# All score groups mirrored from two or more groups back, in the space of weights that are loaded later, and v loaded in eight parts

## The chip, the cores and the metric

The kernel runs on one core of a Trainium2 chip. The metric is device time in microseconds (us), the median of several executions. The core has a matrix engine (PE, whose weight loads are shown as PEld), a vector engine (DVE), a scalar engine (ACT), a general engine (POOL) and a sync engine (SP). SP and POOL also issue DMAs, which 16 DMA engines carry out; those of SP and of POOL go through queues of their own. PSUM is the memory that PE writes its sums to, SBUF the working memory.

## The reference

Eight batches of 2816 rows go through a gated attention, and the result, taken as 22528 tokens, through a mixture of experts:

```python
scores = (1.0 / S) * np.matmul(z, z.transpose(0, 2, 1))   # z: (8, 2816, 64)
attn = np.maximum(scores, 0.0) ** 2
x = u * np.matmul(attn, v)                                # u, v: (8, 2816, 256)
...
h_dense = np.maximum(x @ w1_dense, 0.0)
y_dense = h_dense @ w2_dense
expert_idx = np.argmax(x @ w_gate, axis=1)                # 8 experts
...
y_moe[mask] = gate_w[mask, None] * (np.maximum(x[mask] @ w1[e], 0.0) @ w2[e])
out = y_dense + y_moe
```

Since the scores are z times its own transpose, the matrix `attn` is symmetric: its block (k, i) is the transpose of block (i, k).

## The kernel before, in words

The order of PE, ACT, DVE and SP is written out when the program is built: the code keeps a clock `now` in estimated us, and a small planner (`offer`, `best`, `give`, `run`) hands each vector step to ACT, DVE or POOL by estimated cost and due time. On the chip the engines then follow that order and wait on semaphores only.

**Blocks and groups.** A batch has 22 blocks of 128 rows (`nK = 22`), cut into six groups of 2, 4, 4, 4, 4 and 4 blocks (indices 0 to 5 here). A group's buffer `A[n]` holds `attn` for all 22 key blocks against the group's own blocks, in bf16. There are three such buffers, taken in turn, so group n + 3 reuses the buffer of group n, and scores can run at most two groups ahead (`ahead`, L468).

**Scores.** `scores` (L368) makes two key blocks against the four blocks of a group: two matmuls of 64 x 512, one on the upper and one on the lower half of the array (L383; for the two-block group four key blocks, in four matmuls of 64 x 256). `relu` (L390) then scales and clips from PSUM to a float32 tile `r` (L398 on ACT or L400 on DVE), and a second pass squares into `A` (L411 on ACT, L413 on DVE). PSUM has four pairs of banks for scores, outputs and routing.

**Mirrors.** For `far[n] = [n - 2]`, within a batch, the key blocks that are the columns of group n - 2 are not computed: `far_steps` (L436) issues DMA transposes from `A[n - 2]` on SP (L446), one DMA for each block of group n, with up to four 128 x 128 blocks in each. There are 16 such DMAs in a batch, 128 in all, with 2 x 4 + 3 x 16 = 56 blocks per batch.

**Values.** `av` (L525) makes the output of two blocks i and i + 1 in two passes over the 22 key blocks, in pairs of 64-row matmuls (L552). Between matmuls it lets `fill` run a score call of a group further on. In a group's first pass the key blocks come in the order in which they are expected to be ready. Between the passes `swap_rows` (L503) puts two score calls, or two dummy matmuls `touch` (L496), since the halves of the array change roles there. Every seventh pair of matmuls may issue a mirror DMA (L559). When both passes are done DVE multiplies by u into `pays` (L579), and SP transposes that into `xT` (L581).

**The rest on the queues.** The calendar (`later`, `soon`, L980 to L1008) places steps at ticks, two for each pair of blocks, 22 for a batch: the load of the next batch's z at tick 1, its turning at 6 and 7 (SP), four loads of v at ticks 10, 12, 14 and 16 (`load_v`, L122: a DVE memset of one element, L128, then POOL's DMA, L129), and the weights of the experts (`weights`, L252) three to a batch from batch 2 on. u is loaded by SP (L146) two pairs ahead. Logits (`lg`, L607) for 11 blocks are made five ticks after the last of them is due, from `xT`. POOL scatters each routed block to DRAM (L697).

**Weights.** `wall` holds the weights of the eight experts in SBUF, 2048 elements of each partition for each expert: 1024 for w1, 1024 for w2. They are read only after attention, when the expert stage runs (L909, L912, L917, L932, L933), with DVE copying an expert's weights out of `wall` (L897).

Of the kernel before, what the change touches and what calls it, by code (L numbers as in the profile page):

```python
# [10 lines left out]
BF = mybir.dt.bfloat16  # L11
# [4 lines left out]
P = 128  # L16
# [3 lines left out]
def kernel(  # L20
# [39 lines left out]
    WD = 2 * F + 4 * D  # L60
# [8 lines left out]
    def pool(name, bufs, **kw):  # L69
        return ctx.enter_context(tc.tile_pool(name=name, bufs=bufs, **kw))  # L70
# [3 lines left out]
    aA = pool("aA", 3)  # L74
# [28 lines left out]
    def load_z(b):  # L103
        z_of[b] = zpool.tile([P, nK, dq], BF, name="zr", bufs=1)
        nc.vector.memset(z_of[b][:, 0, 0:1], 0.0)
        nc.gpsimd.dma_start(out=z_of[b][:], in_=z[b].rearrange("(p k) d -> p k d", p=P))

    def turn_z(b, k0, k1):

        if k0 == 0:  # L110
            zn_of[b] = zpool.tile([P, nK, 2, dq], BF, name="zn", bufs=1)
            zT_of[b] = zpool.tile([P, nK, P], BF, name="zT")
        nc.vector.tensor_copy(  # L113
            zn_of[b][:, k0:k1, :, :],
            z_of[b][:, k0:k1, :].unsqueeze(2).to_broadcast([P, k1 - k0, 2, dq]))
        nc.sync.dma_start_transpose(
            out=zT_of[b][:, k0:k1, :],
            in_=zn_of[b][:, k0:k1].rearrange("p k h d -> p (k h d)"))
        if k1 == nK:
            z_there.add(b)  # L120

    def load_v(b, h, parts, gate=True):  # L122
        if h == 0:
            v_of[b] = zpool.tile([P, nK, D], BF, name="vb")
        src = v[b].rearrange("(p k) d -> p k d", p=P)
        k0, k1 = h * nK // parts, (h + 1) * nK // parts
        if gate:
            nc.vector.memset(v_of[b][:, k0, 0:1], 0.0)  # L128
        nc.gpsimd.dma_start(out=v_of[b][:, k0:k1, :], in_=src[:, k0:k1, :])  # L129
        free["pool"] = max(free["pool"], now[0]) + 0.8  # L130


    now = [0.0]
# [130 lines left out]
    A = {}  # L264
    groups = []
    for b in range(B):
        i = 0
# [61 lines left out]
    def until(cond):  # L329

        while cond() is None:
            pick = best()
            assert pick is not None
            now[0] = max(now[0], pick[0][0])
            give(pick)
        now[0] = max(now[0], cond())
        run(now[0])
# [3 lines left out]
        run(now[0])  # L341


    left, far, key_at = {}, {}, {}
    for n, (b, i0, w) in enumerate(groups):
        far[n] = [m for m in (n - 2,) if m >= 0 and groups[m][0] == b]
        turned = {k for m in far[n] for k in range(groups[m][1], groups[m][1] + groups[m][2])}
        ks = [k for k in range(0, nK, 2) if k not in turned]

        left[n] = [tuple(ks[x:x + 4 // w]) for x in range(0, len(ks), 4 // w)]  # L350

    def open_group(n):
        if n not in A:
            A[n] = aA.tile([P, nK, 4 * P], BF, name="A", tag="A")

    def room(n):

# [3 lines left out]
    def take_pair():  # L361
        return pairs.pop(0)[1]
# [68 lines left out]
    def can_turn(n, m):  # L431
        _, i0, w = groups[n]
        ts = [key_at.get((m, k)) for k in range(i0, i0 + w)]
        return None if None in ts else max(ts)

    def far_steps(a):  # L436

        n = a + 2
        if n >= len(groups) or far[n] != [a]:
            return []  # L440
        (b, i0, w), (_, j0, wj) = groups[n], groups[a]

        def step(i):
            assert n - 1 in A
            open_group(n)
            nc.sync.dma_start_transpose(out=A[n][:, j0:j0 + wj, i * P:(i + 1) * P],  # L446
                                        in_=A[a][:, i0 + i, :wj * P])
            if i == w - 1:
                for j in range(wj):
                    key_at[n, j0 + j] = now[0] + 10.0  # L450

        return [(a, lambda i=i: step(i)) for i in range(w)]

    jobs = []

    def fill(n, force=False):

        if jobs and jobs[0][0] <= now[0] and room(1):
            jobs.pop(0)[1]()
            return True  # L460
        m = ahead(n)
        busy = sum(1 for op in todo if op[0] in (1, 4))
        if m is not None and room(1) and busy <= (4 if n < 2 else 2):
            scores(m, left[m].pop(0))
            return True
        return False

    def ahead(n):  # L468

        for m in range(n, min(n + 3, len(groups))):  # L470
            if left[m]:
                return m if groups[m][0] in z_there else None

    def v_at(n, k):

        return 3.3 + 2.6 * (4 * k // nK) if n == 0 else 0.0

    def need(n, k):

        while max(key_at.get((n, k), 9e9), v_at(n, k)) > now[0]:  # L480
            if fill(n):
                continue
            pick = best()
            ts = [t for t, _ in pairs if t > now[0]]
            ts += [max(key_at[n, k], v_at(n, k))] if (n, k) in key_at else []
            assert pick is not None or ts
            if pick is not None and (not ts or pick[0][0] <= min(ts)):
                now[0] = max(now[0], pick[0][0])
                give(pick)
            else:  # L490
                now[0] = min(ts)
        run(now[0])

    turning = []

    def touch(x):  # L496

# [27 lines left out]
    def av(n, i, between):  # L525
        b, i0, w = groups[n]
        if i == i0:
            turning.extend(far_steps(n))
        keep[0] = 0
        if n == 0 and i == i0:  # L530

            fill(n)
            need(n, 0)
        until(lambda: pairs[0][0] if pairs else None)
        ox = take_pair()
        o = banks(ox, "o")
        for p in range(2):
            rest = list(range(nK))
            for x in range(nK):
                k = rest[0]  # L540
                if i == i0 and p == 0:

                    k = min(rest, key=lambda k: (max(key_at.get((n, k), 9e9), v_at(n, k)), k))
                    need(n, k)
                rest.remove(k)
                if n == 0 and i == i0 and p == 0 and x in (12, 14, 16):
                    load_u(2 * (x - 12) // 2, gate=True)
                for h in range(2):
                    r = slice(h * dq, (h + 1) * dq)
                    j = p ^ h  # L550
                    c = (i + j - i0) * P
                    nc.tensor.matmul(out=o[:, j, 0:D], lhsT=A[n][r, k, c:c + P],  # L552
                                     rhs=v_of[b][r, k, :], start=(p == 0 and x == 0),
                                     stop=(p == 1 and x == nK - 1))
# [430 lines left out]
    def soon(t, fn, dur=0.07):  # L985
        at(t, lambda: offer(now[0], 3, {"dve": (dur, lambda eng: fn())}))
# [19 lines left out]
    for e in range(E):  # L1006
# [62 lines left out]
    for q in range(nQ - 2):  # L1069
        t = starts[q + 1] - 1 + LAG  # L1070
# [40 lines left out]
    for s in range(NT - MAYBE + 2):  # L1111
# [4 lines left out]
        if s % 3 == 1 and waiting:  # L1116
# [5 lines left out]
    n = nc.values_load(used[0:1, 0:1], min_val=0, max_val=NH,  # L1122
                       skip_runtime_bounds_check_because="made by the table")
# [34 lines left out]
```

## Time and profile before

| | us |
|---|---|
| median of 3 runs | 882.46 |
| lowest and highest run | 880.53, 889.76 |
| the profiled execution | 887.47 |
| its span, first to last instruction | 885.8 |
| granted PE clock, mean over the span | 0.994 |

The profiled execution is 5.0 us above the median, and 1.7 us of it lie outside the span. In the profile L12 is line 12 of the kernel; a group is written line, engine, operation, out<-in, shape and count, then busy us, mean ns of one, and the engine's idle time ahead of it with what ended it. A name with q (SPq, POOLq) is an engine's queue of instructions that issue DMAs. The DMA share is packet time over 16 engines; packet times can overlap, so it can pass 1.

### The profile page before, as it was taken

To read this page: it belongs to the slowest core of one execution; us is meant where nothing else is said; L and a number is where in the kernel's file an instruction comes from. 1 tells how busy PE (TensorE), PEld (TensorE's weight loads), DVE (VectorE), ACT (ScalarE), POOL (GpSimd) and SP (SyncE) were. 2 spreads that over 40 slices of the span, in tenths; PEclk is the share of its full clock that TensorE was granted. 3 is DMA by queue.
4 is the path that set the end of the run, shared out by engine and by line. 5 is a ranking of instruction groups with operands and counts; after the bars stand their busy time and mean duration, and the time that the engine had idled before them with its cause. 6 is when DMAs were issued, how large, how long until landed. Compare 5 with 4: busy or idle time off the path is not lost.

```text
span 885.8 us, 30592 instructions
## 1 busy us (share of the span) xinstructions
PE 864.5 (98%) x12257; PEld 759.7 (86%) x12257; DVE 701.2 (79%) x1320; ACT 738.6 (83%) x913; POOL 485.2 (55%) x532
## 2 busy tenths in 40 slices
PE   8999999999998999999999999999999999999996
PEld 5788888898886888888888888888888888889996
DVE  7999999998996999999998997656665445546664
ACT  7999998998996998998998997477777777777774
POOL 8203343434533534434434544488888888887665
PEclk9999999999999999999999999999999999999998
DMA  6795997998898899899899896555565555544333
GB/s 148 148 174 117 146 185 145 172 174 170 153 165 168 154 181 190 127 197 198 131 196 172 151 159 112 103 133 128 129 132 122 117 120 121 123 113 110 97 100 82
DMA packets 257871, 127.64 MB, mean 144 GB/s; under 512 B 225470, under 2 KB 232894, under 8 KB 257728
## 3 DMA queue, kind: packets, MB, share of 16 engines
q1 hardware_dynamic: 230112, 70.24, 47.6%
q0 software_dynamic: 27616, 55.44, 29.2%
q8 instruction: 96, 1.57, 0.8%
q14 instruction: 47, 0.39, 0.2%
HBM read 61.54 MB, written 37.16 MB: 111 GB/s over the span
## 4 chain that ended last, share of the span: by engine, by line
PE 73%; DVE 7%; issue 6%; POOL 6%; DMA 4%; ACT 3%; SPq 0%; POOLq 0%; DVEq 0%; ACTq 0%
PE o L552 37%; PE h_ps L909 14%; PE yy L917 13%; PE s L383 8%; POOL out_dram L935 5%; DMA xT<-pays 3%; DVE r L400 2%; DVE A L413 2%; ACT A L411 1%; POOL A L413 1%; PE lg L607 1%; ACT r L398 1%; DVE pays L579 1%; DMA out_dram<-ring,ix 1%; DVE zn L113 1%
## 5 line engine op out<-in xcount | busy, mean ns | idle before, releaser
L552 PE MATMUL o<-vb,A 64*128 64x256 bf16 x7744 | 493.7, 270 | 2.6 <-POOL A L413 1.8
L552 PEld LDWEIGHTS <-A 64*128 64x128 bf16 x7744 | 408.1, 94 | 53.9 <-POOL A L413 3.0
L697 POOL DMA_INDIRECT xs<-pays,pi x176 | 196.9, 1119 | 271.1 <-DVE pi L695 207.1
L398 ACT ACTIVATE r<-s 128x1024 f32<-128x1024 f32 x274 | 270.0, 1011 | 26.1 <-PE s L383 22.1
L411 ACT ACTIVATE A<-r 128x1024 bf16<-128x1024 f32 (+1 forms) x257 | 261.3, 1042 | 5.3 <-DMA A<-A 2.7
L912 ACT ACTIVATE ring<-h_ps 128x1024 bf16<-128x1024 f32 x180 | 183.9, 1023 | 89.2 <-PE h_ps L909 87.3
L413 DVE TENSOR_TENSOR A<-r 128x1024 bf16<-128x1024 f32 x167 | 201.8, 1221 | 5.8 <-DMA A<-A 4.0
L400 DVE TENSOR_SCALAR r<-s 128x1024 f32<-128x1024 f32 (+1 forms) x158 | 190.5, 1214 | 4.3 <-POOL A L413 1.8
L933 DVE SCALAR_TENSOR_TENSOR ring<-yy,me,ring 128x256 f32<-128x256 f32 x180 | 86.8, 482 | 123.0 <-ACT ring L932 86.3
L935 POOL DMA_INDIRECT out_dram<-ring,me x140 | 146.4, 1046 | 39.8 <-issue 23.5
L383 PE MATMUL s<-zT 64*128 64x512 bf16 (+1 forms) x944 | 157.9, 359 | 1.6 <-ACT zT L192 0.6
L917 PEld LDWEIGHTS <-ring 128*128 128x128 bf16 x1440 | 140.0, 98 | 16.2 <-issue 0.3
L917 PE MATMUL yy<-w2d,ring 128*128 128x256 bf16 x720 | 108.0, 273 | 0.1
L917 PE MATMUL yy<-ring 128*128 128x256 bf16 x720 | 108.0, 273 | 0.0
L909 PE MATMUL h_ps<-ring,w1d 128*128 128x256 bf16 x720 | 93.3, 273 | 0.8 <-DVE pays L579 0.8
L909 PE MATMUL h_ps<-ring 128*128 128x256 bf16 (+1 forms) x880 | 93.7, 253 | 0.0
L897 DVE COPY ring<-wall 128x2048 bf16 x110 | 80.7, 748 | 8.6 <-DVE ring L933 4.2
L909 PEld LDWEIGHTS <-ring 128*128 128x128 bf16 x880 | 74.3, 98 | 6.8
L909 PEld LDWEIGHTS <-w1d 128*128 128x128 bf16 x720 | 70.1, 98 | 9.0 <-issue 1.0
L579 DVE TENSOR_TENSOR pays<-o,ut 128x512 bf16<-128x512 f32 x88 | 60.3, 685 | 17.6 <-PE o L552 17.1
L383 PEld LDWEIGHTS <-zT 64*128 64x128 bf16 x944 | 58.0, 94 | 16.0 <-issue 3.4
L932 ACT COPY ring<-yy 128x256 f32<-128x256 f32 x180 | 66.1, 367 | 1.8 <-PE yy L917 1.8
(120 smaller groups left out, 358.0 us busy)
## 6 DMA issues: line engine op xcount, KB each, us to landing
ut<-in_u_dram SPq DMA_DIRECT2D x88, 256.0 KB
vb<-in_v_dram POOLq DMA_DIRECT2D x16, 384.0 KB
vb<-in_v_dram POOLq DMA_DIRECT2D x16, 320.0 KB
wall<-in_moe_w_dram POOLq DMA_DIRECT2D x16, 256.0 KB
xs<-pays,pi POOLq DMA_INDIRECT x176
zr<-in_z_dram POOLq DMA_DIRECT2D x7, 352.0 KB
out_dram<-ring,me POOLq DMA_INDIRECT x140
A<-A SPq DMA_TRANSPOSE x128
```

The lines of the kernel that those rows point to most:

```text
L383: nc.tensor.matmul(out=s[:, h, y * c:(y + 1) * c], lhsT=zT[r, k + h, :], rhs=zT[r, i0:i0 + w, :], start=True, stop=True)
L398: nc.scalar.activation(r[:, :, :c], s[:, :, :c], AF.Relu, scale=1.0 / S)
L400: nc.vector.tensor_scalar(out=r[:, :, :c], in0=s[:, :, :c], scalar1=1.0 / S, scalar2=0.0, op0=ALU.mult, op1=ALU.max)
L411: nc.scalar.activation(a, r, AF.Square)
L413: (nc.gpsimd if eng == "pool" else nc.vector).tensor_mul(a, r, r)
L552: nc.tensor.matmul(out=o[:, j, 0:D], lhsT=A[n][r, k, c:c + P], rhs=v_of[b][r, k, :], start=(p == 0 and x == 0), stop=(p == 1 and x == nK - 1))
L697: ins = nc.gpsimd.indirect_dma_start(out=xs, out_offset=bass.IndirectOffsetOnAxis(ap=pi[:], axis=0), in_=pays[:, g % (2 * G), 0:ROW].bitca ...
L909: nc.tensor.matmul(out=h_ps[:, f, hs, :], lhsT=w1(c, f), rhs=xT[:, hs, c, :], start=(c == 0), stop=(c == 1))
L912: nc.scalar.activation(h, h_ps[:].rearrange("p f h t -> p f (h t)"), AF.Relu)
L917: nc.tensor.matmul(out=y[:, k, :], lhsT=h[:, f, j * P:(j + 1) * P], rhs=w2(f), start=(f == 0), stop=(f == 3))
L933: nc.vector.scalar_tensor_tensor(out=ys, in0=y[:, 1, :], scalar=me[:, j, 0:1], in1=yd, op0=ALU.mult, op1=ALU.add)
L935: ins = nc.gpsimd.indirect_dma_start(out=out, out_offset=bass.IndirectOffsetOnAxis(ap=ids[j], axis=0), in_=ys, in_offset=None, bounds_chec ...
```

## The change

A group is now mirrored from every earlier group of its batch that is two or more back. The mirrors from exactly two back go into the group's own buffer, as before; those from further back go to slots in `wall` that belong to the experts 3 to 7, whose weights come later. Batch 6 uses the slots of experts 7 and 6 alone, batch 7 none. One DMA now carries all the blocks between two groups, 16 (8 from the two-block group), and the layout of a mirrored piece is one run of blocks. A score call of the group that will reuse a buffer waits, in the planner, until the mirrors from that buffer are issued and expected to be read (`read_at`), and two mirror DMAs are spaced by `turn_at`. `A` of the two-block group is packed. z is loaded one tick sooner, v in eight parts at ticks 13 to 20, and the weights at the ends of the batches from 3 on.

```diff
+    spare = wall[:].rearrange("p e w -> p (e w)")
+    mirror = {(2, 5): (E - 1) * WD, (1, 5): (E - 2) * WD, (1, 4): (E - 3) * WD,
+              (0, 4): (E - 4) * WD, (0, 5): (E - 4) * WD + 8 * P, (0, 3): (E - 5) * WD + 2 * F}
+
+    def slots(b):
+        if b < B - 2:
+            return list(mirror)
+        return [(2, 5), (1, 5)] if b == B - 2 else []
...
-        far[n] = [m for m in (n - 2,) if m >= 0 and groups[m][0] == b]
+        far[n] = [m for m in range(max(n - 5, 0), n - 1)
+                  if groups[m][0] == b and (m == n - 2 or (m % 6, n % 6) in slots(b))]
...
     def open_group(n):
         if n not in A:
-            A[n] = aA.tile([P, nK, 4 * P], BF, name="A", tag="A")
+            while turning and turning[0][0] <= n - 3:
+                turning.pop(0)[1]()
+            A[n] = aA.tile([P, nK, 4 * P], BF, name="A", tag="A")[:]
+            w = groups[n][2]
+            if w < 4:
+                A[n] = A[n].rearrange("p k c -> p (k c)")[:, :nK * w * P]
+                A[n] = A[n].rearrange("p (k c) -> p k c", k=nK)
...
+    def turned_to(a, n):
+        _, j0, wj = groups[a]
+        w = groups[n][2]
+        if a == n - 2:
+            flat = A[n].rearrange("p k c -> p (k c)")
+            return flat[:, j0 * w * P:(j0 + wj) * w * P]
+        x = mirror[a % 6, n % 6]
+        return spare[:, x:x + w * wj * P]
+
+    def block(n, k, c):
+        _, i0, w = groups[n]
+        for a in far[n]:
+            _, j0, wj = groups[a]
+            if j0 <= k < j0 + wj:
+                x = c * wj + k - j0
+                return turned_to(a, n)[:, x * P:(x + 1) * P]
+        return A[n][:, k, c * P:(c + 1) * P]
...
     def far_steps(a):
-        def step(i):
-            assert n - 1 in A
-            open_group(n)
-            nc.sync.dma_start_transpose(out=A[n][:, j0:j0 + wj, i * P:(i + 1) * P],
-                                        in_=A[a][:, i0 + i, :wj * P])
...
+        _, j0, wj = groups[a]
+        def step(n):
+            _, i0, w = groups[n]
+            if n == a + 2:
+                assert a + 1 in A
+                open_group(n)
+            nc.sync.dma_start_transpose(
+                out=turned_to(a, n).rearrange("p (x c) -> p x c", c=P),
+                in_=A[a][:, i0:i0 + w, :].rearrange("p k c -> p (k c)"))
+            turn_at[0] = now[0] + 0.17 * w * wj
+            read_at[a] = now[0] + 1.5 + 0.19 * w * wj
+            for j in range(wj):
+                key_at[n, j0 + j] = now[0] + 7.0
+
+        return [(a, lambda n=n: step(n), n) for n in range(a + 2, min(a + 6, len(groups)))
+                if a in far[n]]
...
             if left[m]:
+                if m == n + 2 and (turning and turning[0][0] <= m - 3 or read_at.get(m - 3, 0.0) > now[0]):
+                    return None
                 return m if groups[m][0] in z_there else None
...
-                    nc.tensor.matmul(out=o[:, j, 0:D], lhsT=A[n][r, k, c:c + P],
+                    nc.tensor.matmul(out=o[:, j, 0:D], lhsT=block(n, k, i + j - i0)[r],
...
-                if x % 7 == 3 and turning:
-                    t = can_turn(turning[0][0] + 2, turning[0][0])
+                if x % 7 == 3 and turning and turn_at[0] <= now[0]:
+                    t = can_turn(turning[0][2], turning[0][0])
...
-            soon(t + 1, lambda b=b: load_z(b + 1))
-            soon(t + 6, lambda b=b: turn_z(b + 1, 0, nK // 2), 0.4)
-            soon(t + 7, lambda b=b: turn_z(b + 1, nK // 2, nK), 0.4)
-            for h in range(4):
-                soon(t + 10 + 2 * h, lambda b=b, h=h: load_v(b + 1, h, 4))
+            soon(t, lambda b=b: load_z(b + 1))
+            soon(t + 5, lambda b=b: turn_z(b + 1, 0, nK // 2), 0.4)
+            soon(t + 6, lambda b=b: turn_z(b + 1, nK // 2, nK), 0.4)
+            for h in range(8):
+                soon(t + 13 + h, lambda b=b, h=h: load_v(b + 1, h, 8))
 
-    ts = [b * nK + x for b in range(1, B) for x in (0, 5, 18)][3:]
+    ts = [b * nK + x for b in range(3, B - 2) for x in (15, 18, 21)]
+    ts += [(B - 2) * nK + x for x in (14, 16, 18, 20, 21)]
+    ts += [(B - 1) * nK + x for x in (0, 5, 10, 15)]
```

More of the change, by code (lines that the diff above doesn't have):

```diff
@@ L434, in can_turn @@
         return None if None in ts else max(ts)
-    def far_steps(a):
[L438 to L441, printed above, removed]
-        def step(i):
-            assert n - 1 in A
-            open_group(n)
-            nc.sync.dma_start_transpose(out=A[n][:, j0:j0 + wj, i * P:(i + 1) * P],
-                                        in_=A[a][:, i0 + i, :wj * P])
[L448 to L452, printed above, removed]
+    def turned_to(a, n):
[14 more added lines that the diff above has]
+        return A[n][:, k, c * P:(c + 1) * P]
+    def far_steps(a):
+        _, j0, wj = groups[a]
[13 more added lines that the diff above has]
+                if a in far[n]]
+    turning = []
+    turn_at = [0.0]
+    read_at = {}
     jobs = []
@@ L492, in need @@
         run(now[0])
-    turning = []
     def touch(x):
@@ L550, in av @@
                     j = p ^ h
-                    c = (i + j - i0) * P
-                    nc.tensor.matmul(out=o[:, j, 0:D], lhsT=A[n][r, k, c:c + P],
+                    nc.tensor.matmul(out=o[:, j, 0:D], lhsT=block(n, k, i + j - i0)[r],
                                      rhs=v_of[b][r, k, :], start=(p == 0 and x == 0),
@@ L996 @@
         if b + 1 < B:
-            soon(t + 1, lambda b=b: load_z(b + 1))
-            soon(t + 6, lambda b=b: turn_z(b + 1, 0, nK // 2), 0.4)
-            soon(t + 7, lambda b=b: turn_z(b + 1, nK // 2, nK), 0.4)
-            for h in range(4):
-                soon(t + 10 + 2 * h, lambda b=b, h=h: load_v(b + 1, h, 4))
-    ts = [b * nK + x for b in range(1, B) for x in (0, 5, 18)][3:]
+            soon(t, lambda b=b: load_z(b + 1))
[6 more added lines that the diff above has]
+    ts += [(B - 1) * nK + x for x in (0, 5, 10, 15)]
+    assert len(ts) == 2 + 2 * E
     soon(ts.pop(0), lambda: dense(w1d, moe_w1_dense, 2))
```

## The prediction

> **What bounds the kernel now.** I read the page first, then the stages, then single matmuls. The page:
>
> ```profile
> span 885.8 us, 30592 instructions
> ...
> PE 864.5 (98%) x12257; PEld 759.7 (86%) x12257; DVE 701.2 (79%) x1320; ACT 738.6 (83%) x913; POOL 485.2 (55%) x532
> ...
> PE 73%; DVE 7%; issue 6%; POOL 6%; DMA 4%; ACT 3%; SPq 0%; POOLq 0%; DVEq 0%; ACTq 0%
> PE o L552 37%; PE h_ps L909 14%; PE yy L917 13%; PE s L383 8%; POOL out_dram L935 5%; DMA xT<-pays 3%; DVE r L400 2%; DVE A L413 2%; ACT A L411 1%; POOL A L413 1%; PE lg L607 1%; ACT r L398 1%; DVE pays L579 1%; DMA out_dram<-ring,ix 1%; DVE zn L113 1%
> ```
>
> PE is busy 98% of the span, and 73% of the chain that ended last is PE. A stage of attention (busy us of PE, PEld, DVE, ACT, POOL with their counts, then granted clock, DMA share and rate):
>
> ```profile
> 320.00:395.00 75.00, 74.91 (x1277) 65.73 (x1275) 72.07 (x126) 70.25 (x78) 32.45 (x34) 1.00 1.04 175
> ```
>
> There PE, DVE (72.07 of 75), ACT (70.25) and the DMA engines (share 1.04) are all nearly full. Which one sets the pace is seen in PE's order of time (start, length, engine, line):
>
> ```profile
> 354.04 2.80 PE L552 MATMUL o<-vb,A 64*128 64x256 bf16 x48
> 356.66 0.40 PE L383 MATMUL s<-zT 64*128 64x512 bf16 x2
> 356.88 0.40 PE L552 MATMUL o<-vb,A 64*128 64x256 bf16 x4
> 357.09 0.17 PE L499 MATMUL d<-ones 64*128 64x8 bf16 x1
> 357.11 0.64 PE L383 MATMUL s<-zT 64*128 64x512 bf16 x4
> 357.58 1.49 PE L552 MATMUL o<-vb,A 64*128 64x256 bf16 x24
> ```
>
> 48 value matmuls take 356.66 - 354.04 = 2.62 us: two run side by side on the halves of the array, and each pair costs 0.109 us. A score call of a four-block group costs 356.88 - 356.66 = 0.22 us (two calls: 357.58 - 357.11 = 0.47). Nothing is idle between, so PE's own work is the attention's time. The Trainium skill ("Perfetto Trace Analysis", section Identifying the Most-Contended Engine) says that matmul busy time is a bad measure of PE's headroom and that weight-load busy time is a good one; by that, the 65.73 of 75 would leave 12% in PE. The spacing decides against it here.
>
> **Scores removed.** Per batch, group 3 takes 2 more key blocks from mirrors, group 4 takes 6 and group 5 takes 10: 18 key blocks, in 9 calls of two. Batches 0 to 5 lose 9 calls, batch 6 loses 4, batch 7 none: 58 of 432 (the built order has 944 - 828 = 116 score matmuls fewer). On PE 58 x 0.216 = 12.5 us, all on the path. What goes with them on the other engines:
>
> ```profile
> L398 ACT ACTIVATE r<-s 128x1024 f32<-128x1024 f32 x268 | 266.5, 1020 | 25.4 <-PE s L383 21.5 <-POOL A L413 1.0 <-DVE A L413 0.6
> L411 ACT ACTIVATE A<-r 128x1024 bf16<-128x1024 f32 x251 | 257.9, 1052 | 5.3 <-DMA A<-A 2.7 <-DVE r L400 1.3 <-DVE vb L128 0.8
> L413 DVE TENSOR_TENSOR A<-r 128x1024 bf16<-128x1024 f32 x166 | 201.1, 1224 | 5.8 <-DMA A<-A 4.0 <-ACT r L398 1.0
> L400 DVE TENSOR_SCALAR r<-s 128x1024 f32<-128x1024 f32 x156 | 189.1, 1221 | 4.1 <-POOL A L413 1.6 <-PE s L383 1.2
> ```
>
> 116 passes of 1.02 to 1.22 us, some 130 us over two engines, which only gives them slack.
>
> **Swaps without scores.** With fewer calls to spread, more passes end with no score to run, and two dummies stand in. The built order has 16 such pairs of dummies, against 8:
>
> ```profile
> 345.15 0.42 PE L499 MATMUL d<-ones 64*128 64x8 bf16 x2
> 345.42 0.83 PE L552 MATMUL o<-vb,A 64*128 64x256 bf16 x12
> ```
>
> 345.42 - 345.15 = 0.27 us each: 8 x 0.27 = 2.2 us back.
>
> **Mirrors added.** SP issues 70 mirror DMAs for 128, but they carry 128 blocks per batch for 56. Their load:
>
> ```profile
> q1 hardware_dynamic: 230112, 70.24, 47.6%
> ```
>
> 0.476 x 885.8 us x 16 / 230112 = 29.3 ns of one engine per packet. A block is 32 KB in 256-byte packets, so 128 of them: 0.234 us of all 16 engines (an estimate). 72 more blocks cost 16.9 us per batch, nearly all in the first six block pairs of a batch. Batch 4's first six, before:
>
> ```profile
> 299.00:305.00 6.00, 6.00 (x105) 5.44 (x101) 5.66 (x10) 5.97 (x7) 3.32 (x3) 1.00 0.92 151
> 305.00:311.00 6.00, 6.00 (x113) 5.09 (x111) 5.90 (x11) 5.89 (x8) 2.66 (x2) 1.00 1.08 196
> 311.00:317.00 6.00, 6.00 (x103) 4.84 (x101) 5.79 (x11) 6.00 (x7) 2.75 (x3) 1.00 1.03 170
> 317.00:323.00 6.00, 6.00 (x107) 5.19 (x103) 5.44 (x16) 5.71 (x7) 1.49 (x2) 1.00 1.48 140
> 323.00:329.00 6.00, 6.00 (x101) 5.24 (x98) 5.97 (x10) 5.34 (x7) 2.42 (x3) 1.00 1.05 214
> 329.00:335.00 6.00, 6.00 (x105) 5.44 (x103) 5.96 (x8) 6.00 (x7) 2.14 (x3) 1.00 1.11 202
> ```
>
> The shares (packet times can overlap, so they pass 1) sum to 6.67 x 6 = 40.0 us in 36. With 16.9 more, and the v part of 2.8 (last fence) gone to later, 54.1 us, or 1.50: just the highest share a stretch here shows, 1.48. So the queue is full for half a batch, with little backlog, and the mirrors themselves have time: each is read two groups on, over 12 us after its issue. Behind them on SP stand the u loads and the xT turns. In the trace:
>
> ```profile
> 256.92 1.21 SPq L581 DMA_TRANSPOSE xT<-pays  x1
> 258.29 7.18 SPq L446 DMA_TRANSPOSE A<-A  x4
> 265.57 0.53 SPq L146 DMA_DIRECT2D ut<-in_u_dram  x1
> 266.14 1.21 SPq L581 DMA_TRANSPOSE xT<-pays  x1
> ```
>
> Four mirrors held SP for 7.18 us, while v was loading too. Then DVE, ACT (the 2.7 us in its row above) and PE waited:
>
> ```profile
> 270.37 1.22 DVE L413 TENSOR_TENSOR A<-r 128x1024 bf16<-128x1024 f32 x1 [3.22 <-DMA A<-A]
> ```
> ```profile
> 273.52 0.20 PE L607 MATMUL lg<-wg,xT 128*128 128x8 bf16 x2 [4.19 <-DMA xT<-pays]
> ```
> ```profile
> PE lg L607 <- DMA xT<-pays: 6.6, 4, 4.2
> ```
> ```profile
> 273.00:279.00 6.00, 5.38 (x68) 4.17 (x70) 4.27 (x12) 3.28 (x5) 2.68 (x3) 0.72 0.76 177
> ```
>
> The third row is the waits' list (total, times, longest). 4.19 us, and (1 - 0.72) x 6 = 1.7 us of lowered clock behind it. This collision is what moving v removes: v now starts at block 13, when the mirrors (issued by block 11 in the built order) are out. The other three waits, 2.4 us, I count half gone: 1.2. The rest of the queue gets no price (bounds: 0 and one 3.22 us wait per batch, a rival below): the new guards hold the next scores back until a mirror is read.
>
> **v in eight parts.** The last part now goes at block 20, mid of the batch's last pair; call that T. In the built order its DVE memset stands behind one relu of a score that PE makes at once: T + 0.25 + 1.22 + 0.06, about T + 1.6. Then:
>
> ```profile
> 267.09 0.06 DVE L128 MEMSET vb<- 128x1 bf16 x1
> ```
> ```profile
> 267.46 0.57 POOL L129 DMA_DIRECT2D vb<-in_v_dram  x1 [0.21 <-issue]
> ```
> ```profile
> 345.48 0.06 DVE L128 MEMSET vb<- 128x1 bf16 x1
> ```
> ```profile
> 347.57 0.60 POOL L129 DMA_DIRECT2D vb<-in_v_dram  x1
> ```
> ```profile
> q0 software_dynamic: 176, 0.47, 63.1%
> ```
>
> 0.3 to 2.0 us to the issue (with a scatter between), 0.6 to issue. The last row is of 347.5 to 351.9 us (63.1% x 4.4 = 2.8 us of all engines): a 384 KB part issued by 348.17 was in by 351.9, 3.7 us. Half the size takes between 1.9 and 3.7. So it lands from T + 4.4 to T + 7.9. PE first needs it after two scores, 22 pairs, one score, 19 pairs and two scores: 0.47 + 2.40 + 0.22 + 2.07 + 0.44 = T + 5.6. The wait is 0 to 2.3 us at each of 7 batch starts; nearest is the first pair of rows (no scatter between), so I take 0.2: 1.4 us. The Trainium skill ("DMA: Bandwidth & Descriptors", section Anatomy of one DMA) fits such a load as 2.0 us and its bytes at 436 GB/s: an estimate of 2.45 us for 192 KB, T + 5.0, no wait and 1.4 us less in the sum; for 384 KB it gives 2.9 where the trace has 3.7. z one block earlier, and the weights in fewer batches, lie beside PE work: nothing.
>
> **The sum.** Profiled execution 887.5 (1.7 outside the span), 5.0 above the median 882.46, and its 4.19 + 1.7 = 5.9 us stall explains that; so I step down to the median by 5.0. 887.5 - 12.5 + 2.2 - 5.0 - 1.2 + 1.4 = 872.4, so 872.
>
> **The rivals.**
> - Mirrors read late (slower). An A buffer may not be written until the mirror DMAs have read it, now up to four of them. The guard assumes 4.5 us for 16 blocks; a backlog beyond that puts the 3.22 us wait at the head of DVE or ACT, their relus queue behind, the score banks fill and PE stops. Once per batch with mirrors (six), 3.2 each: 872 + 19 = 891. It decides when a 16-block mirror takes over some 5 us to land. For: share 1.50. Against: v is away, and groups get their first scores a pair or two after the last mirror.
> - The last v part is late, by 1.5 us at 7 starts: 10.5 for my 1.4, so 881.
> - ACT and DVE, not PE, pace attention: 130 us over two engines, 65 off: some 817. This is also where the weight-load rule would point. Against it the 0.109 us spacing.
>
> **How the numbers follow.** Forecast 0.62 (its own range 867 to 878), mirrors late 0.14, v late 0.20, ACT and DVE 0.04. About 1% (8.8 us) can be told from no change: under 873.6 is faster. The forecast lies under it in about 7 of 10, with the last rival 0.47; slower is the first rival in most of its weight, 0.13; the rest 0.40. Range 866 to 886: the forecast, v late, and the mild end of mirrors late.
>
> **What would show it.** Score calls 374; attention's last value matmul some 10 us earlier, beside the stalls; no wait of PE on xT over 1 us; PE's waits at the first pass of a batch on v under 0.5 us; ACT and DVE several points less busy; waits of A on A<-A below 5 us in sum. I am wrong if those last waits come in every batch, or if SP's 16-block issues hold up u so that DVE's gate waits.

## The result, and the profile after

The changed kernel takes 915.83 us (median of 4 runs, 914.45 to 918.48); the kernel before took 886.11 us on the same chip (4 runs, 880.53 to 892.04). The ratio is 1.0338, interval 1.0254 to 1.0422: slower by some 30 us, where 872 was forecast and 866 to 886 was the range. Ratios here are of fast runs alone, so they can differ a little from the quotient of two medians.

The page of the kernel after, with its span, the engines, SP's DMA queue and the chain that ended last:

```profile
span 913.0 us, 30155 instructions
...
PE 864.6 (95%) x12150; PEld 754.5 (83%) x12150; DVE 649.2 (71%) x1305; ACT 676.0 (74%) x840; POOL 491.3 (54%) x559
...
q1 hardware_dynamic: 287648, 85.44, 56.0%
...
PE 40%; DMA 13%; POOL 9%; issue 9%; DVE 5%; ACT 2%; SPq 1%; POOLq 0%; DVEq 0%; ACTq 0%
...
L428 ACT ACTIVATE A<-r 128x1024 bf16<-128x1024 f32 x215 | 220.6, 1055 | 51.1 <-DMA wall<-A 26.1
...
L430 DVE TENSOR_TENSOR A<-r 128x1024 bf16<-128x1024 f32 (+1 forms) x151 | 180.9, 1209 | 52.0 <-DMA wall<-A 24.7
```

The work went as forecast: DVE and ACT have 8 to 9 points less to do, and 57,536 packets were added to q1. But the span grew by 27.2 us, PE went from 73% of the chain to 40%, and DMA from 4% to 13%. The two squares (L428, L430; before L411, L413) stood idle 5 us each before, and now 51 and 52 us.

The list of waits of the kernel after (who waited for what: total us, times, longest):

```profile
ACT A L428 <- DMA wall<-A: 26.1, 10, 6.6
...
DVE A L430 <- DMA wall<-A: 24.7, 8, 4.9
...
DVE A L430 <- DMA A<-A: 18.2, 6, 3.7
...
ACT A L428 <- DMA A<-A: 16.3, 6, 3.3
...
PE o L594 <- DMA vb<-in_v_dram: 11.4, 7, 2.1
```

The first four rows are one thing: a square may not write its `A` buffer until the mirrors out of the buffer's previous group have read it. They sum to 85.3 us in 30 waits, against 6.7 before. ACT and DVE mostly stood at the same mirror: the 30 waits end at 17 moments in six batches. The last row is v: late at all seven batch starts.

How such a wait gets to PE, in batch 4. SP in order of time (start, length), then DVE, then PE:

```profile
341.85 2.44 SPq L482 DMA_TRANSPOSE wall<-A  x1
...
349.23 3.48 SPq L482 DMA_TRANSPOSE A<-A  x1
```
```profile
346.69 1.23 DVE L430 TENSOR_TENSOR A<-r 128x1024 bf16<-128x1024 f32 x1 [4.47 <-DMA wall<-A]
...
356.95 1.23 DVE L430 TENSOR_TENSOR A<-r 128x1024 bf16<-128x1024 f32 x1 [3.24 <-DMA A<-A]
358.10 1.22 DVE L417 TENSOR_SCALAR r<-s 128x1024 f32<-128x1024 f32 x1
```
```profile
359.37 0.40 PE L594 MATMUL o<-vb,wall 64*128 64x256 bf16 x4 [1.81 <-DVE pi L737]
```

By these rows the mirror that SP issued at 349.23 had read its buffer at 356.9, 7.7 us on; one issued at 341.85 had taken 4.8. The square stood at the head of DVE until then, with the relu behind it, which empties a pair of banks of scores. That relu ended at 358.10 + 1.22 = 359.32, and PE, which needs a free pair of banks to begin the next output, went on at 359.37. (PE's row names DVE's `pi`, because the profile puts a wait down to the last semaphore; a value matmul reads nothing of `pi`, and the relu is what ended there.)

The stages of batch 4 (they begin 2.3 us after the batch's first value matmul, those shown of before 6.2 us after it; busy us of PE, PEld, DVE, ACT, POOL, then clock, DMA share, rate):

```profile
307.00:313.00 6.00, 4.95 (x82) 4.38 (x82) 4.24 (x6) 3.94 (x5) 2.27 (x3) 1.00 1.03 182
313.00:319.00 6.00, 6.00 (x105) 5.44 (x102) 5.57 (x8) 5.56 (x7) 2.72 (x2) 1.00 1.56 147
319.00:325.00 6.00, 6.00 (x116) 5.07 (x112) 3.74 (x7) 4.62 (x5) 1.92 (x2) 1.00 0.80 175
325.00:331.00 6.00, 4.30 (x67) 3.19 (x63) 5.86 (x12) 4.90 (x7) 1.71 (x2) 1.00 1.05 214
331.00:337.00 6.00, 6.00 (x103) 4.91 (x104) 5.76 (x17) 5.98 (x8) 1.93 (x2) 1.00 1.01 192
337.00:343.00 6.00, 6.00 (x107) 5.54 (x103) 5.22 (x7) 4.41 (x5) 1.93 (x2) 1.00 1.13 182
343.00:349.00 6.00, 4.61 (x84) 4.35 (x82) 2.31 (x3) 2.29 (x3) 0.74 (x1) 1.00 1.16 211
349.00:355.00 6.00, 6.00 (x114) 5.30 (x115) 2.82 (x8) 3.61 (x4) 3.71 (x5) 1.00 1.22 234
355.00:361.00 6.00, 3.92 (x81) 3.48 (x78) 4.02 (x10) 4.06 (x5) 1.35 (x2) 1.00 1.00 175
```

The first six shares sum to 6.58 x 6 = 39.5 us, as before (40.0), where the forecast had put 54.1 into them. The DMA engines held no larger a share in those 36 us than before, though a part of v had been moved out of them (queue q0: 1.37 MB for 1.96). SP's queue q1 ran 16,957 packets in them for 13,420: 3,537 more, where the 72 added blocks have 72 x 128 = 9,216. The rest slid behind them (10,771 packets for 5,685 in the next 30 us), and the two mirrors above past the moment at which their buffers were wanted.

Where the 27.2 us of span went. Attention, from the first value matmul to the end of the last, takes 575.9 us for 551.8, 24.1 more: scores -12.5 and dummies +2.2, as forecast; PE idle 35.4 us for 9.7, +25.7; and a clock of 0.50 for 20.5 us, for 6.8 before, of which half is lost: +6.8. That makes 22.2; the other 1.9 were not placed. Another 0.2 lie at the start. The last 2.9 lie behind PE's last matmul, where the span goes on for 10.0 us, for 7.1 before; e8 and e15 below have the same 10.0. No term of the forecast holds these 2.9, and what makes them wasn't traced. The clock after a wait on v, from the stages:

```profile
86.00:92.00 6.00, 4.10 (x43) 3.09 (x44) 4.43 (x7) 3.00 (x4) 1.44 (x1) 0.75 1.22 154
```

### The profile page after: what moved, and what is told of

The parts are those of the page before. It is cut to its first block, busy times and chain, and to the rows that moved or that the text cites. A ratio compares the mean times of both kernels' runs of the same rounds, so it can differ in the third digit from the quotient of the medians.

```text
span 913.0 us, 30155 instructions
## 1 busy us (share of the span) xinstructions
PE 864.6 (95%) x12150; PEld 754.5 (83%) x12150; DVE 649.2 (71%) x1305; ACT 676.0 (74%) x840; POOL 491.3 (54%) x559
## 3 DMA queue, kind: packets, MB, share of 16 engines
q8 instruction: 95, 1.56, 0.7%
## 4 chain that ended last, share of the span: by engine, by line
PE 40%; DMA 13%; POOL 9%; issue 9%; DVE 5%; ACT 2%; SPq 1%; POOLq 0%; DVEq 0%; ACTq 0%
PE h_ps L951 13%; PE yy L959 12%; PE o L594 12%; DMA wall<-A 6%; POOL out_dram L977 5%; DMA A<-A 2%; DMA vb<-in_v_dram 2%; POOL xs L739 2%; PE s L400 2%; DVE A L430 2%; DMA out_dram<-ring,ix 1%; ACT A L428 1%; POOL vb L129 1%; DVE r L417 1%; ACT r L415 1%
## 5 line engine op out<-in xcount | busy, mean ns | idle before, releaser
L594 PE MATMUL o<-vb,A 64*128 64x256 bf16 x6816 | 438.3, 272 | 14.3 <-DMA vb<-in_v_dram 11.4
L594 PEld LDWEIGHTS <-A 64*128 64x128 bf16 x6816 | 358.7, 95 | 59.9 <-issue 14.3
L739 POOL DMA_INDIRECT xs<-pays,pi x176 | 190.2, 1081 | 278.3 <-DVE pi L737 215.8
L415 ACT ACTIVATE r<-s 128x1024 f32<-128x1024 f32 x243 | 241.6, 1022 | 62.7 <-PE s L400 60.7
L428 ACT ACTIVATE A<-r 128x1024 bf16<-128x1024 f32 x215 | 220.6, 1055 | 51.1 <-DMA wall<-A 26.1
L430 DVE TENSOR_TENSOR A<-r 128x1024 bf16<-128x1024 f32 (+1 forms) x151 | 180.9, 1209 | 52.0 <-DMA wall<-A 24.7
L977 POOL DMA_INDIRECT out_dram<-ring,me x140 | 148.1, 1058 | 44.4 <-issue 22.2
L417 DVE TENSOR_SCALAR r<-s 128x1024 f32<-128x1024 f32 (+1 forms) x131 | 154.5, 1186 | 16.7 <-PE s L400 15.3
L400 PE MATMUL s<-zT 64*128 64x512 bf16 (+1 forms) x828 | 137.1, 360 | 2.4 <-ACT r L415 1.3
L594 PE MATMUL o<-vb,wall 64*128 64x256 bf16 x928 | 72.4, 274 | 12.0 <-DVE pi L737 8.4
```

The source lines that it names most:

```text
L400: nc.tensor.matmul(out=s[:, h, y * c:(y + 1) * c], lhsT=zT[r, k + h, :], rhs=zT[r, i0:i0 + w, :], start=True, stop=True)
L415: nc.scalar.activation(r[:, :, :c], s[:, :, :c], AF.Relu, scale=1.0 / S)
L417: nc.vector.tensor_scalar(out=r[:, :, :c], in0=s[:, :, :c], scalar1=1.0 / S, scalar2=0.0, op0=ALU.mult, op1=ALU.max)
L428: nc.scalar.activation(a, r, AF.Square)
L430: (nc.gpsimd if eng == "pool" else nc.vector).tensor_mul(a, r, r)
L594: nc.tensor.matmul(out=o[:, j, 0:D], lhsT=block(n, k, i + j - i0)[r], rhs=v_of[b][r, k, :], start=(p == 0 and x == 0), stop=(p == 1 and x ...
```

## The experiments

Two causes were on the table: buffers held by mirrors, and v late. Behind the first stood three explanations: SP's or the planner's order, a guard (`read_at`) that is too short, or the load itself. All edits are to the kernel after; lines of experiments can differ by a few. "A" is the summed wait of the squares on mirrors and "v" PE's wait on v, both in the profiled execution. Every ratio is to the kernel before on the same chip.

| run | us | before | ratio | A | v |
|---|---|---|---|---|---|
| e1_mirror_elsewhere | 947.21 | 928.19 | 1.017 (1.010 to 1.024) | 0 | 12.3 |
| e2_v_block10 | 977.76 | 928.19 | 1.051 (1.045 to 1.057) | 126.0 | 1.3 |
| e3_two_back | 948.70 | 928.19 | 1.022 (1.016 to 1.027) | 0 | 16.6 |
| e4_guard_5us | 960.87 | 928.19 | 1.035 (1.028 to 1.042) | 56.2 | 13.0 |
| e5_before_again, one run | 882.94 | | | 2.0 | 0 |
| e6_after_again | 919.79 | 884.78 | 1.040 (1.029 to 1.050) | 71.3 | 12.4 |
| e7_elsewhere_v10 | 926.09 | 884.78 | 1.045 (1.034 to 1.055) | 0 | 1.0 |
| e8_two_back_v10 | 880.87 | 884.78 | 0.996 (0.992 to 1.000) | 0 | 0 |
| e9_quarter | 900.04 | 886.39 | 1.011 (1.006 to 1.016) | 0.7 | 17.5 |
| e10_quarter_v10 | 896.67 | 886.39 | 1.010 (1.007 to 1.014) | 20.8 | 0 |
| e11_three_back_v10 | 894.93 | 886.39 | 1.005 (1.001 to 1.010) | 21.4 | 1.8 |
| e12_three_back_v12 | 885.40 | 886.39 | 0.996 (0.992 to 1.000) | 0.6 | 3.9 |
| e13_quarter_v11 | 880.99 | 889.01 | 0.994 (0.990 to 0.998) | 18.0 | 2.3 |
| e14_three_back_v11 | 888.64 | 889.01 | 1.001 (0.997 to 1.004) | 7.1 | 2.1 |
| e15_two_back_v11 | 881.93 | 889.01 | 0.993 (0.990 to 0.996) | 0 | 0.6 |

**First set: each suspected wait by itself.** The first reads the mirrors from expert 0's place in `wall`, which is kept at zero, so no buffer is held under the same load; it leaves the mirrored part of attention out:

```diff
+    nc.vector.memset(wall[:, 0, :], 0.0)
...
-                in_=A[a][:, i0:i0 + w, :].rearrange("p k c -> p (k c)"))
+                in_=wall[:, 0, 0:w * wj * P])
```

> The changed kernel, but every mirror DMA reads a run of zeros (expert 0's place in the weights, which then stays zero) in place of the earlier group's buffer; so the mirrored part of the attention is zero. Same number, size, order and destination of DMAs, same order on every engine. Theory W (the squares wait to write into a buffer that a mirror DMA still reads): the waits of A on mirrors, 85 us on ACT and DVE in the changed kernel, go to nearly 0, the waits of PE at the start of group 4 go with them, and the time falls from 916 to 885-895. Theory D (the DMA load itself is what costs: mirrors, u, xT and v land late): the load is the same, so 910 or more. Theory V (v's last part): its 7 waits of about 1.6 us stay in either case.

The second moves v ahead, the third leaves the far mirrors out (their scores are computed again), the fourth lengthens the guard:

```diff
-                soon(t + 13 + h, lambda b=b, h=h: load_v(b + 1, h, 8))
+                soon(t + 10 + h, lambda b=b, h=h: load_v(b + 1, h, 8))
```

> The changed kernel with v's eight parts at blocks 10 to 17, three blocks sooner, and nothing else changed. Theory V: the 7 waits of PE on v (11.4 us) go to 0, with the lowered clock behind some of them, and the time falls to 895-905. Theory W: v now loads while the last mirrors of a batch do, these are read later, the waits of A on mirrors grow from 85 us to 100 or more, and the time stays at 910 or rises. Theory D: the same load in the same batch, 910-916.

```diff
     def slots(b):
-        if b < B - 2:
-            return list(mirror)
-        return [(2, 5), (1, 5)] if b == B - 2 else []
+        return []
```

> The changed kernel with mirrors from two groups back alone, as before, but in DMAs of up to 16 blocks, with the new calendar of v, z and weights: 432 score calls again, 56 mirrored blocks a batch. Theory W: the farther mirrors are what holds the buffers, so the waits of A on mirrors fall below 15 us; what is left over before is v, 7 waits of 1 to 2 us, so 886-898. If the DMA of 16 blocks itself is the cost, the waits of A on mirrors stay above 40 us and the time stays above 900.

```diff
-            read_at[a] = now[0] + 1.5 + 0.19 * w * wj
+            read_at[a] = now[0] + 6.5 + 0.19 * w * wj
```

> The changed kernel with the guard 5 us longer: the planner takes a mirror of 16 blocks as read 9.5 us after its issue and not 4.5, so the next scores into that buffer are placed later. Theory W with a guard that is only too short: the waits of A on mirrors fall from 85 us to below 30, and the time to 890-905. If SP issues the mirrors much later than the planner thinks, 5 us are not enough and the waits stay above 60 us with the time within 1% of 916; the same if the scores, pushed later, come too late for PE.

This chip was slower: the kernel before took 928 us on it. The kernel after was not run there, so e1 to e4 are set against each other, and against after's ratio only loosely. The chip's extra time lies behind attention: 361 to 368 us from the last value matmul to the end, for 324 in the kernel before and 327 in the kernel after on their chip. So the attention stages can be set side by side with some care: e1 564.4 us, e2 605.2, e3 571.1, e4 575.6, for 575.9 in the kernel after and 551.8 in the kernel before.

Four things follow. With no buffer held, e1 loses the squares' waits and some 11 us of attention; the waits on v stay. A longer guard doesn't mend it (1.035, A still 56.2 us): so planning for a later read doesn't take the cost away. e3 is slower than the kernel before although its q1 carries no more (227,040 packets for 230,112) and no square waits on a mirror; the late v is the only wait on a DMA that its list has, and e8 below tests that by moving v alone. And v ahead, among the mirrors, is the worst of the four. The waits of e2:

```profile
ACT A L428 <- DMA wall<-A: 39.2, 10, 7.7
DVE A L430 <- DMA A<-A: 36.5, 6, 10.2
```

and one of them, in order of time:

```profile
150.72 1.23 DVE L430 TENSOR_TENSOR A<-r 128x1024 bf16<-128x1024 f32 x1 [5.86 <-DMA A<-A]
151.86 1.22 DVE L417 TENSOR_SCALAR r<-s 128x1024 f32<-128x1024 f32 x1
...
153.13 0.61 PE L594 MATMUL o<-vb,wall 64*128 64x256 bf16 x4 [4.21 <-DVE pi L737]
```

v no longer waits (1.3 us), but it takes from the mirrors what it gains, and PE stops for 4.21 us behind the same square and relu.

**Second set: both kernels again, and both causes cut at once.** e5 is the kernel before and e6 the kernel after, without an edit.

> The kernel before, unchanged, for a profile beside the others of this batch of runs. No theory tells anything else than the reference time, and an attention stage of about 552 us.

> The changed kernel, unchanged, beside the others of this batch. Ratio to before 1.03 to 1.04 and an attention stage of about 576 us.

They repeat the result. e7 joins the edits of e1 and e2, e8 those of e3 and e2.

> The changed kernel with both cuts: mirrors read the zeros of expert 0's place (so no buffer is held), and v's eight parts come at blocks 10 to 17. If the held buffers and the late v are all that was wrong with the forecast, the attention stage comes to 543 us or less and the ratio to 0.985-0.995: PE's removed score work shows. Theory D (the load on the DMA engines, which is all still there and now has v in its middle): waits of PE on xT or u or on mirrors arriving take the place, ratio above 1.01.

> Mirrors from two groups back alone (as before, in DMAs of up to 16 blocks), and v's eight parts at blocks 10 to 17. If late v is what the calendar costs, the 7 waits on v are gone and the ratio is 0.99 to 1.005. If the 16-block DMA or the other moves of the calendar (z, weights) cost too, the ratio stays above 1.01.

e7 has hardly any of the two waits (0 and 1.0), and is as slow as the kernel after. Its SP around 130 us, and PE and DVE at what SP issued or issued late:

```profile
129.63 2.60 SPq L116 DMA_TRANSPOSE zT<-zn  x1
...
135.88 5.11 SPq L484 DMA_TRANSPOSE A<-wall  x1
```
```profile
139.28 0.39 PE L402 MATMUL s<-zT 64*128 64x256 bf16 x1 [6.05 <-DMA zT<-zn]
```
```profile
DVE pays L623 <- DMA ut<-in_u_dram: 23.7, 3, 11.0
...
PE s L402 <- DMA zT<-zn: 16.1, 5, 6.0
...
PE lg L651 <- DMA xT<-pays: 8.8, 3, 6.0
```

A turn of z issued by 132.23 landed at 139.28, and the issue of one mirror held SP for 5.11 us. With no buffer held and v among the mirrors, the delay comes out at what SP issues next: u, z's turn, xT. That is not so with v out of the way: e1 lists no wait on u or on z's turn, and 1.5 us on xT. So the load can reach PE by more than one way, and this run can't say how much goes by each. e8, with the 16-block DMAs but only the mirrors from two back and v at blocks 10 to 17, has no wait on a DMA in attention, and each of batches 1 to 6 takes 67.2 us or 67.3: at four a batch, the long DMAs themselves cost nothing that shows. It differs from e3 by v's place alone (1.022 there, on another chip), so by these two the late v is what e3 pays for.

**Third set: the load alone.** e9 keeps every instruction of the kernel after in its order, and the planner's guards, but a far mirror moves one row of blocks for four. The rest of each slot, zeroed once by POOL, leaves that part of attention out; the zeroing puts the first value matmul at 18.59 us for 10.59 in e6, 8.0 later:

```diff
+    nc.gpsimd.memset(wall[:, 3:8, :], 0.0)
...
+            m = w if n == a + 2 else 1
             nc.sync.dma_start_transpose(
-                out=turned_to(a, n).rearrange("p (x c) -> p x c", c=P),
-                in_=A[a][:, i0:i0 + w, :].rearrange("p k c -> p (k c)"))
+                out=turned_to(a, n)[:, 0:m * wj * P].rearrange("p (x c) -> p x c", c=P),
+                in_=A[a][:, i0:i0 + m, :].rearrange("p k c -> p (k c)"))
```

> The changed kernel, but each mirror from three or more groups back moves only the blocks of the first of the target's four rows (4 of 16, 2 of 8); the rest of its slot stays zero, so that part of the attention is left out. Number and order of DMAs and of all engines' work unchanged; 74 mirrored blocks a batch in place of 128, and the buffers are still read by DMAs issued at the same places. Theory D (the added load is what makes mirrors late, and the held buffers are only where it shows): waits of A on mirrors fall from 71 us to below 20; the 7 waits on v stay (10-13 us); attention 578 -> 550-558, ratio 1.005-1.015. Theory W (the order: buffers are asked for before mirrors can be through, whatever the load): waits of A stay above 40 us, ratio above 1.025.

Its list of waits has one wait of a square on a mirror, 0.7 us, where the kernel after has 85.3 in 30 (the second row is the zeroing at the start; e6 has a wait of 1.3 us in that place):

```profile
PE o L596 <- DMA vb<-in_v_dram: 17.5, 7, 5.4
...
PE o L596 <- POOL A L431: 10.0, 2, 9.0
...
ACT A L429 <- DMA wall<-A: 0.7, 1, 0.7
```

The DMA queue rows over 66 us of batch 4 (packets, MB, share), of e9 and of the kernel after:

```profile
q1 hardware_dynamic: 20859, 7.41, 67.7%
```
```profile
q1 hardware_dynamic: 27728, 9.15, 81.7%
```

This run bears most on the cause: same order, same planner's guards, lighter mirrors, and the waits are gone. But it changes two things, since a mirror that reads one row also holds less of its buffer. Of the 30 squares that waited in the kernel after, 17 have no semaphore of a DMA left to wait for in e9, as its trace lists them. The other 13 list the same ones as in the kernel after, and only one of these waits, for 0.7 us: there the lighter load alone did it. Without its own 8.0 us e9 takes 892.0, against e6's 919.79: 27.8 us for the load together with what it holds. e1 parts the two as far as two chips compare: whole load and nothing held, attention 564.4 us, where e6 has 578.5, the kernel after 575.9 and e9 558.9. With v out of the way, then, most of the load's cost reached PE through held buffers. SP's issuing alone is an unlikely rival: it takes SP 48 to 53 us in each of batches 1 to 5 of the kernel after, and 46 to 50 in the kernel before. What stays in e9 is v.

e10 is e9 with v at 10 to 17; e11 and e12 keep mirrors up to three back, with v at 10 to 17 and at 12 to 19:

```diff
-    mirror = {(2, 5): (E - 1) * WD, (1, 5): (E - 2) * WD, (1, 4): (E - 3) * WD,
-              (0, 4): (E - 4) * WD, (0, 5): (E - 4) * WD + 8 * P, (0, 3): (E - 5) * WD + 2 * F}
+    mirror = {(2, 5): (E - 1) * WD, (1, 4): (E - 3) * WD, (0, 3): (E - 5) * WD + 2 * F}
...
-        return [(2, 5), (1, 5)] if b == B - 2 else []
+        return [(2, 5)] if b == B - 2 else []
```

> The same with v's eight parts at blocks 10 to 17. Theory D: with the load light again, v can come early without a collision, no wait of PE above 1 us is left, and the removed score calls show: attention 533-540, ratio 0.98-0.99, what the forecast had. Theory W: waits of A as in the run before, ratio above 1.01.

> Mirrors from two and three groups back, 96 blocks a batch, whole, and v at blocks 10 to 17; 10 key blocks fewer a batch, 5 score calls. A search for a version that beats both, and a point between loads of 56 (ratio 0.996) and 128 blocks. If the load decides with a threshold, and 96 lies below it: 6.5 us of score work gone, ratio 0.988-0.993. Above it: zT, u and xT come late, ratio 1.01 or more.

> The same with v at blocks 12 to 19, one block before the place where the last part was late. If the lateness of v is a matter of some 2 us, the last part is in time here, and the mirrors have two blocks more without v: ratio at or below that of v at 10 to 17. If v is still late: 7 waits of 0.5 us or more on v.

At v 10 to 17 both collide again (A 20.8 and 21.4 us); at 12 to 19 the three-back kernel hardly does (0.6, with 3.9 on v). e10 was expected at 0.98 to 0.99 and misses it. None of the three beats the kernel before by more than its interval.

**Fourth set: v between the two.** v at blocks 11 to 18, with the light mirrors (zeroed by DVE in smaller pieces), with three back and with two back:

```diff
-                soon(t + 13 + h, lambda b=b, h=h: load_v(b + 1, h, 8))
+                soon(t + 11 + h, lambda b=b, h=h: load_v(b + 1, h, 8))
```

> As e9 (each mirror from three or more groups back moves only the first of the target's four rows, the rest of its slot is zero, so that part of the attention is left out), with v's eight parts at blocks 11 to 18, and the zeros written by DVE at the start in place of POOL, whose 9 us held up the first batch in e9 and e10. The load theory: light load and v neither late nor early leaves no wait of PE above 1 us in batches 1 to 5; each takes about 65.7 us, attention 532-536, ratio 0.982-0.990: the removed score work of the forecast shows in full. If the order of the kernel costs something of its own: batches above 67 us, ratio 0.995 or more.

> Mirrors from two and three groups back, whole, 96 blocks a batch, v at blocks 11 to 18. Between e11 (v at 10: mirrors, zT and buffers late, 1.005) and e12 (v at 12: v late by about 1 us at four batch starts, 0.996). If there is room between them: no wait of either kind above 1 us, ratio 0.988-0.993. If not: 0.996 or more.

> Mirrors from two groups back alone, 56 blocks a batch, v at blocks 11 to 18. At this load v's place should not matter between 10 and 11: ratio 0.994-0.999, as with v at 10. Beside it the run before tells what 5 score calls fewer a batch are worth: 0.4 to 0.7% if nothing waits.

e13 keeps PE's work of the change without the load, and leaves the same part of attention out as e9. Of its batches 1 to 7 all but batch 4 (71.97) take 65.6 to 66.5 us, two of them in these stages:

```profile
90.00:156.00 66.00, 65.63 (x1134) 57.19 (x1130) 57.41 (x110) 52.97 (x57) 29.96 (x31) 1.00 1.04 176
156.00:222.00 66.00, 65.81 (x1138) 57.02 (x1136) 56.35 (x110) 53.16 (x59) 28.24 (x31) 1.00 1.05 174
```

PE is full with ACT at 53 of 66 us: PE's own work sets the pace. Its first value matmul starts 4.1 us later than the kernel after's, for the zeroing (14.57 against 10.47); without that its ratio is 0.9941 - 4.1 / 889 = 0.9895, and the forecast was 872.4 / 882.46 = 0.9886. That they come so close is in part chance: batch 4 is some 6 us too long and the tail behind PE 2.9, and stalls of the kernel before are gone. e13's squares still wait 18.0 us in sum, so that sum is not a price: it costs only where it reaches PE.

e14 finds no room between e11 and e12: 1.001, with batches 4 and 5 at 70.6 and 70.4 us for 66.4 to 66.6 in batches 1 to 3.

e15 computes everything and has the lowest ratio of the kernels that do, 0.993 (0.990 to 0.996); e8 and e12, at 0.996, lie at the edge of its interval. Its attention in stages of 75 us, the first after the start and two further on:

```profile
90.00:165.00 75.00, 75.00 (x1281) 65.86 (x1277) 71.96 (x127) 71.56 (x78) 36.70 (x34) 1.00 0.91 159
...
315.00:390.00 75.00, 74.91 (x1281) 65.92 (x1278) 71.64 (x129) 70.93 (x77) 36.49 (x37) 1.00 0.93 173
390.00:465.00 75.00, 74.91 (x1276) 65.54 (x1273) 71.41 (x131) 70.46 (x77) 36.88 (x38) 1.00 0.98 171
```

PE is idle for 0.2 us in 225, and for 3.7 us in all of attention, 9.7 before. The gain is not in fewer scores, since it computes those of the kernel before, but in the stalls: in the runs that the ratio counts the kernel before took 881.93 to 895.16 us beside it, e15 881.37 to 884.08. The best of both are alike; e15 comes near its best in each run.

## Why the prediction was wrong, step by step

- **PE sets the pace, 0.109 us per pair.** Right: e13's and e15's stages. The rival of ACT and DVE (817 us) fell: they had 7 to 9% less to do and the kernel didn't follow. By the rule of the Trainium skill ("Perfetto Trace Analysis", section Identifying the Most-Contended Engine), which takes weight-load busy time as a measure of PE's headroom, e15's 65.9 of 75 would leave 12% too; PE stood idle there for 0.2 us of 225.
- **Scores -12.5, dummies +2.2.** Right. A batch without stalls takes 67.2 us with two-back mirrors (e8) and 65.6 to 65.9 with all of them (batches 1, 2 and 5 of e13): 1.3 to 1.6 a batch; forecast were 10.3 us over six full batches, 1.7 each.
- **The mirrors' queue priced at 0: the step that failed.** The prediction summed the first six shares to 1.50, held that against "the highest share a stretch here shows, 1.48", and concluded that "the queue is full for half a batch, with little backlog". 1.48 was one stretch of 6 us among shares of 0.92 to 1.11; the mean over 36 us was 1.11. After, a stretch reached 1.56, but the mean over 36 us was again 1.10. Moved through attention in steps of 2 us, no stretch of 36 us passes 1.24 in the two runs of the kernel before and 1.22 in the two of the kernel after, and the highest found in any trace here is 1.33 (e7, 526 to 562). So the 1.50 that the sum put there was not to be had: what can be held for half a batch was read from a peak. The load, with the buffers that it holds, cost 27.8 us (e6 against e9). The first rival named the right mechanism and the right point, a landing beyond some 5 us (4.8 and 7.7 above), but counted one wait in a batch; there were 17 such moments in six, about three a batch, and in each of the six, which is the prediction's own sign of being wrong. It should have had the larger chance, as a sum that ends at the highest share ever seen leaves no room.
- **v in eight parts, 1.4 us.** Mis-sized. The forecast took the bound of the quiet landing, 0.2 us a start; the waits are 1.05 to 2.14 us each, 11.4 in all, inside the range it gave (0 to 2.3) and near the rival's 1.5. The price is larger than the waits: e9 without its zeroing takes 892.0, where 886.4 - 10.3 = 876.1 was due, so about 16 us with lowered clock and the tail, net of the stalls of before that are gone. e13, with v two blocks sooner, is back at 881.0 - 4.1 = 876.9, on another chip.
- **Moving v removes the stall on xT.** Right by itself: PE's waits on xT are 0.6 us in all (before 6.6). But the rivals were priced as if they excluded each other. Both came, and they are coupled: v later than the mirrors is late, v among them delays them (e2, e7). The Trainium skill ("DMA: Bandwidth & Descriptors", section Issuing engines are not separate DMA queues) says that DMAs of all issuing engines run on the same 16 DMA engines and interleave. e2 agrees: v is issued by POOL, the mirrors by SP, and with v moved among them the waits on v are 1.3 us (11.4 in the kernel after) and those of the squares 126.0 (85.3; both on another chip).

On one chip the account closes by its making: 886.4 - 10.3 + 15.9 + 27.8 = 919.8, e6's time. The split between v and load is e9's, and its 27.8 holds load and holding together; effects of the two together are not additive in general.

**Open.** Single batches stay 4 to 7 us longer than their neighbours: 1 and 4 of e10, 4 of e13, 4 and 5 of e14. Each has waits of PE of 1.4 to 3.2 us and a lowered clock behind them; what shifts the order there wasn't traced. How the cost parts between the load and the holding is known only from e1, on another chip. Whether a fourth `A` buffer would hide the load wasn't tried.

## What to carry to other kernels

Price a burst of transfers by the share that the DMA engines held over a stretch as long as the burst, not by the best short stretch, and count as late whatever doesn't fit. Then ask which buffer the late transfer still holds, and what is queued behind the instruction that wants it: a square on DVE stopped PE here, through a relu and a bank of scores. Saved matmuls that are paid for with transfers are worth it only up to the load that fits; here the kernel that saved no more of them than the kernel before, and spaced its transfers, had the lowest ratio of those that compute all.

## What the runs showed of the hardware

- The clock fell behind gaps of 2 us. In attention it falls to 0.50 for 3.41 us at a time, or a whole multiple of that, in the clock records of the kernels before and after; 3.41 us at half the clock lose 1.7. The kernel after has five such falls, one of them double, the kernel before two. After the wait of 1.95 us on v that ended at 87.90 the stage 86 to 92 has a clock of 0.75; but after 2.08 us idle in 355 to 361 the clock stayed at 1.00. The Trainium skill ("TensorE: Matmul & The Clock Gate", section Part 1: The HAM clock gate) gives an idle window of about 3.4 us before the clock halves, and calls the window free-running. The length of a fall agrees with that window; the gap of 1.95 us is shorter than it, and no run here shows why one gap of 2 us lowers the clock and another doesn't.
- Issuing one transposing DMA of 16 blocks held SP for 2.4 to 5.1 us in the rows above, and from 1.3 to 7.5 us in the whole of the kernel after; four of four blocks had taken 7.18 before.
- One chip took 928.19 us for the kernel that took 884.78 to 889.01 on the others. The difference lies behind attention (361 to 368 us there in e1 to e4, 324 to 328 elsewhere), so total times are set side by side on one chip only.
